# One weight load cut in two, and summing matmuls spread over four column tiles, in a fused adaLN + linear attention + GEGLU kernel

## The chip, the cores and the metric

The kernel runs on 1 core of one Trainium2 chip. The metric is device time in microseconds (us), median over runs. The profile of a kernel is one execution, and its span (first to last instruction) is usually 2.1 to 2.2 us shorter than the device time of the same run. PE is TensorE's matmuls, PEld its weight loads, DVE VectorE, ACT ScalarE, SP the engine whose queue issues the DMAs.

## The reference, cut to what matters

```python
mod = (silu(c) @ w_mod).reshape(1, 6, 1, -1)      # six rows of 1024
sa, ca, ga, sb, cb, gb = ...
h = layernorm(x) * (1 + ca) + sa                  # x: 2048 x 1024, bf16
x = x + ga * linear_attention(h, wqkv, wo)        # 32 heads, D = 1024
h = layernorm(x) * (1 + cb) + sb
x = x + gb * (gelu(h @ w_gate) * (h @ w_up) @ w_down)   # F = 3584
```

Two kinds of work come from `mod`. `sa` and `ca` are needed at once, before the first `k` matmul, as one value per partition. `ga`, `sb`, `cb` and `gb` are needed later, two of them (`ga`, `gb`) as rows copied to all partitions.

Of the kernel before, what the change touches and what calls it, by code (L numbers as in the profile page):

```python
# [7 lines left out]
ACTF = mybir.ActivationFunctionType  # L8
ALU = mybir.AluOpType

P = 128
# [203 lines left out]
def bass_adaLN_cond__linear_attn_block__geglu_ffn__prompt_kernel(  # L215
# [13 lines left out]
    scr_row = nc.dram_tensor("scr_row", [3, 4, 512], f32).ap()  # L229
    scr_rd = nc.dram_tensor("scr_rd", [NSG, 2, HPG, NG * (SGW // 2)], f32).ap()  # L230
    with ExitStack() as es:
# [3 lines left out]
        ps_all = es.enter_context(nc.psum_tensor("ps_all", [P, 8 * 512], f32))  # L235
# [75 lines left out]
        ONES, SILF, C8, CT, CHALF, THC, SILUT = (_small[k] for k in ("ones", "silf", "c8", "cT", "chalf", "thc", "siluT"))  # L311
# [5 lines left out]
        def r_sm(name):  # L317
            return [(SMO[name], SMO[name] + SMSZ[name], name)]
# [73 lines left out]
        def pr(b):  # L392
            return [(b * 2048, (b + 1) * 2048)]
# [7 lines left out]
        sch = Sched()  # L401
        T, A, V, G, Q = PE_, ACT_, DVE_, POOL_, SP_
# [11 lines left out]
        def pset_writer(b, o):  # L414
            for t_ in pr(b):
                sch.ps.set_writer(t_[0], t_[1], o)
# [30 lines left out]
        def w_dma(dst, off, name, kind, c0, c1, dc0=0, dc1=NDC):  # L447
            return sch.dma(Q, lambda e: e.dma_start(dst[:, dc0:dc1, c0:c1], wqkv_v[:, dc0:dc1, kind * D + c0:kind * D + c1]),  # L448
                           wr=[t_ for dc in range(dc0, dc1) for t_ in r_w(off, name, dc, c0, c1)], note=f"{name}.{dc0}.{c0}")

        def wmq_dma(q, ts=(0, 1)):
            for t in ts:
                sch.dma(Q, lambda e, t=t: e.dma_start(WMQ[q][:, :, t, :], wm_v[:, :, t * D + q * 256:t * D + (q + 1) * 256]),  # L453
                        wr=r_wmq(q, t), note=f"wmq{q}.{t}")
# [10 lines left out]
        x_dma(3, 4)  # L465
        for q in range(1, 4):
            wmq_dma(q)
            for d0, d1 in ((2, 4),) if q == 1 else ((2 * q, 2 * q + 1), (2 * q + 1, 2 * q + 2)):
                w_dma(WK, OFF_WK, "wk", 1, 0, D, d0, d1)
        w_dma(WV, OFF_WV, "wv", 2, 0, 512, 0, 4)  # L470
        w_dma(WV, OFF_WV, "wv", 2, 0, 512, 4, 8)
# [7 lines left out]
               rd=r_sm("c8") + r_sm("ident"), pwr=pr(4))  # L479
# [4 lines left out]
               rd=r_sm("thc") + r_sm("chalf"), wr=r_sm("siluT"))  # L484
# [152 lines left out]
        def mod_rows(parts):  # L637
            for k0, n, bank, src in parts:
                o = None
                for h in range(2):  # L640
                    for j in range(n):
                        ap, rng = src(k0 + j, h)
                        o = sch.op(T, lambda e, h=h, j=j, ap=ap, bank=bank: e.matmul(  # L643
                            ps_all[32 * j:32 * (j + 1), bank * 512:(bank + 1) * 512], ONES[:, :], ap, start=(h == 0), stop=(h == 1)),
                            rd=rng + r_sm("ones"), pwr=(pr(bank) if h == j == 0 else ()), note=f"modr{k0}.{h}.{j}")
                pset_writer(bank, o)

        def mod_store(n, bank, dst, rng, row):
            sch.op(A, lambda e: e.activation(dst[0:32 * n, :], ps_all[0:32 * n, bank * 512:(bank + 1) * 512], ACTF.Copy),
                   prd=pr(bank), wr=rng, note=f"mrow{row}")  # L650
            return sch.dma(Q, lambda e: e.dma_start(scr_row[row, 0:n, :], dst[0:32 * n:32, :]), rd=rng, note=f"mrow{row}.st")

        def hl_src(k, h):
            return HL[k // 4][:, k % 4, h, :], r_hl(k, h, h + 1)
# [57 lines left out]
        def nb():  # L712
            b = bank_i[0] % bank_i[1]
            bank_i[0] += 1
            return b
# [123 lines left out]
        for c_ in range(4):  # L839
            for vc, jg in (((0, 0), (1, 0)), ((0, 1), (1, 1)), ((2, 0), (2, 1)), ((3, 0), (3, 1)))[c_]:  # L840
                b = nb()
# [58 lines left out]
        for c_ in range(4, NCH):  # L900
# [23 lines left out]
            for jg in range(2):  # L924
                b = nb()
# [3 lines left out]
            for jg in range(2):  # L929
                b = nb()  # L930
# [3 lines left out]
            if c_ == 13:  # L934
                assert mdone[0] == 48 and not late
                b2_ = nb()
                mod_rows(((0, 2, 4, hl_src), (2, 4, b2_, hl_src)))
                o_r = mod_store(2, 4, MROW[0], r_2k(OFF_ROW, "mrow0"), 0)
                row_load(GAB, R_GAB, 0, 0, "gab", o_r)
                o_r = mod_store(4, b2_, MROW[1], r_2k(OFF_ROW + 2048, "mrow1"), 1)  # L940
                for dst, nt, a0 in ((SBT, "sbT", 0), (CBT, "cbT", 2)):
                    sch.dma(Q, lambda e, dst=dst, a0=a0: e.dma_start(dst[:, :], scr_row[1, a0:a0 + 2, :].rearrange("a (b p) -> p (a b)", p=P)),
                            wr=r_sm(nt), deps=[o_r], note=nt)
# [262 lines left out]
        def gb_rows():  # L1206
            mod_rows(((0, 2, 7, lambda j, h: (HLG[:, j, h, :], r_hlg(j, h))),))
            o_ = mod_store(2, 7, MRG, [(OFF_GAB, OFF_GAB + 2048, "mrg")], 2)
            row_load(GBB, R_GBB, 2, 0, "gbb", o_)
# [107 lines left out]
```

## The kernel before: what the change touches

At the start, one DMA queue (SP) brings in x, four "quarters" of the columns of `w_mod` for `sa` and `ca` (`wmq`), and the k weight (`wk`). A quarter holds two 128-row blocks `dc` of the contraction: TensorE can run the `k` matmuls of a `dc` only when the `wk` rows of that `dc` are there and the quarter's `wmq` have given `sa` and `ca` for it.

```python
x_dma(0, 1); x_dma(1, 2); wmq_dma(0, (1,)); x_dma(2, 3); wmq_dma(0, (0,))
w_dma(WK, OFF_WK, "wk", 1, 0, D, 0, 2)                       # wk, first quarter, one load
x_dma(3, 4)
for q in range(1, 4):
    wmq_dma(q)                                               # two loads of 512 KB
    for d0, d1 in ((2, 4),) if q == 1 else ((2 * q, 2 * q + 1), (2 * q + 1, 2 * q + 2)):
        w_dma(WK, OFF_WK, "wk", 1, 0, D, d0, d1)             # q == 1: one load of 512 KB
# ... (wv, x, wq)
# TensorE, in program order:
k_tiles([2, 3], [(0, 0), (0, 1), (1, 0), (1, 1)])            # first use of wk of the second quarter
# ...
mod_cols(2, 4)                                               # third quarter: waits for its wmq
# ...
mod_cols(3, 4)                                               # fourth quarter: waits for the last wmq
# ... the rest of the kernel
```

`mod_cols` is 32 matmuls of one column. The later rows of `mod` are summed on VectorE per partition, and TensorE adds over the partitions with a matmul by a 128 x 32 matrix of ones. I call the part of the array that such an output of 32 partitions uses (128*32 in the traces) a column tile; there are four, `j` picks one, and `h` adds the high and the low bf16 half of the sum.

```python
def mod_rows(parts):
    for k0, n, bank, src in parts:
        for h in range(2):
            for j in range(n):                 # n = 2: two column tiles; n = 4: all four
                ap, rng = src(k0 + j, h)
                o = sch.op(T, lambda e, ...: e.matmul(
                    ps_all[32 * j:32 * (j + 1), bank * 512:(bank + 1) * 512], ONES[:, :], ap,
                    start=(h == 0), stop=(h == 1)), ...)
        pset_writer(bank, o)

def mod_store(n, bank, dst, rng, row):
    sch.op(A, lambda e: e.activation(dst[0:32 * n, :], ps_all[0:32 * n, bank * 512:(bank + 1) * 512], ACTF.Copy), ...)
    return sch.dma(Q, lambda e: e.dma_start(scr_row[row, 0:n, :], dst[0:32 * n:32, :]), ...)
```

There are two sites: one in the k/v phase (a group of n = 2, then one of n = 4) and one at the end of the first feed-forward group (n = 2).

## Time and profile before

| | before |
|---|---|
| device time, median (3 runs) | 839.39 us (838.2 to 840.23) |
| profiled span | 835.7 us |
| TensorE busy | 829.8 us |

From the page of the kernel before: the span, the busy time of each engine, and the shares of the chain of work that ended last.

```profile
span 835.7 us, 11352 instructions
...
PE 829.8 (99%) x4189; PEld 384.2 (46%) x4189; DVE 512.3 (61%) x898; ACT 336.2 (40%) x555; POOL 36.7 (4%) x91
...
PE 97%; SPq 2%; DMA 1%; issue 0%; DVE 0%
```

The chain is TensorE (PE) nearly all the way. Here it is in order of time, kernel before; the columns are start, duration and what the chain went through.

```profile
17.27 1.51 SPq L453
18.83 5.91 DMA wmq<-in_w_mod_dram
24.78 0.95 PE ps_all L602 x32
...
151.80 0.97 PE ps_all L643 x12
...
348.98 0.54 PE ps_all L643 x4
```

Up to 24.78 us the chain is SP's issuing and then the last `wmq` load. From 24.78 us on, at the 32 matmuls of `mod_cols(3)` (L602), it is PE. I call this moment the *resume*. The ones matmuls (L643) are two pieces of that PE chain, 0.97 and 0.54 us.

All of PE's waits, kernel before (total us, times, longest):

```profile
PE ps_all L478 <- POOL bmask L429: 2.1, 1, 2.1
PE ps_all L602 <- DMA wmq<-in_w_mod_dram: 0.6, 2, 0.4
PE ps_all L680 <- DVE h1T L565: 0.5, 1, 0.5
```

The timeline of the kernel before around the second quarter's first `k` matmul, and the `mod_cols` of the third and fourth quarter; in brackets the idle time in front, with what seems to have ended it:

```profile
16.30 0.38 DVE L565 TENSOR_SCALAR h1T<-h1T,modt 128x384 bf16<-128x384 bf16 x1
...
17.02 2.53 PE L680 MATMUL ps_all<-wk,h1T 128*128 128x512 bf16 x11 [0.49 <-DVE h1T L565]
...
20.57 0.95 PE L602 MATMUL ps_all<-siluT,wmq 128*128 128x1 bf16 x32
...
24.78 0.95 PE L602 MATMUL ps_all<-siluT,wmq 128*128 128x1 bf16 x32 [0.21 <-DMA wmq<-in_w_mod_dram]
```

The list of DMA issues, limited to the window of the second quarter's `wk` load (issued at 8.62 us), kernel before; the last column is us from issue to landing:

```profile
wk<-in_A_wqkv_dram SPq DMA_DIRECT2D x1, 512.0 KB, 8.3
```

The load lands at 16.92 us. DVE's multiply for the first `dc` is done at 16.68, and PE starts at 17.02. So the profile's "DVE" as releaser is a near miss: the load came last.

The weight load of that first matmul, in the timeline of all engines, kernel before, and the last instruction of VectorE, whose end I call the *end* below:

```profile
16.99 2.07 PEld L680 LDWEIGHTS ps_all<-wk,h1T 128*128 128x128 bf16 x11 [0.64 <-DVE h1T L565]
...
833.54 0.22 DVE L1164 TENSOR_TENSOR xall<-ps_all,xall 128x64 bf16<-128x64 f32 x1
```

The ones matmuls of the kernel before, by form (minimum, median and maximum ns of one, then first and last start):

```profile
L643 PE MATMUL ps_all<-hl,ones x12: 379/379/391, 151.7 to 152.4; 128*32 128x512 bf16 x12
L643 PE MATMUL ps_all<-hlg,ones x4: 379/384/390, 348.9 to 349.1; 128*32 128x512 bf16 x4
```

### The profile page before, as it was taken

How to read it: one execution, taken by the hardware profiler on the slowest of the kernel's cores; microseconds unless marked ns; L12 is line 12 of the kernel's file. 1: busy time of each engine (PE TensorE's matmuls, PEld its weight loads, DVE VectorE, ACT ScalarE, POOL GpSimd, SP SyncE). 2: the span in 40 equal slices, each digit the busy share in tenths (PEclk: the TensorE clock that was granted, in tenths of full speed). 3: DMA queues.
4: the chain of work that ended last, by engine and by line, in shares of the span. 5: the costliest groups of instructions: out<-in, count | busy, mean ns of one | idle time of the engine just before them, and what ended most of it. 6: DMA issues, size and time to landing. Idle time of an engine off the chain costs nothing.

```text
span 835.7 us, 11352 instructions
## 1 busy us (share of the span) xinstructions
PE 829.8 (99%) x4189; PEld 384.2 (46%) x4189; DVE 512.3 (61%) x898; ACT 336.2 (40%) x555; POOL 36.7 (4%) x91
## 2 busy tenths in 40 slices
PE   8999999999999999999999999999999999999998
PEld 4544444444444444444444444444444444444445
DVE  6778877687785567753566665355556535555512
ACT  2357777446423354420444442045554104455300
POOL 2012111000200000000000000000000000000000
PEclk9999999999999999999999999999999999999999
DMA  9984323239796779180555533055553305555000
GB/s 284 332 240 120 83 76 84 70 88 227 151 234 194 227 210 275 26 188 26 158 151 151 152 101 75 20 158 152 151 151 102 76 20 161 153 154 143 7 19 26
DMA packets 184102, 113.22 MB, mean 135 GB/s; under 512 B 35560, under 2 KB 175080, under 8 KB 183024
## 3 DMA queue, kind: packets, MB, share of 16 engines
q1 hardware_dynamic: 184032, 112.50, 49.9%
q8 instruction: 33, 0.54, 0.3%
q14 instruction: 21, 0.17, 0.1%
q10 hardware_dynamic: 16, 0.00, 0.0%
HBM read 100.67 MB, written 4.47 MB: 126 GB/s over the span
## 4 chain that ended last, share of the span: by engine, by line
PE 97%; SPq 2%; DMA 1%; issue 0%; DVE 0%
PE ps_all L1157 23%; PE ps_all L1129 23%; PE ps_all L1132 23%; PE ps_all L680 12%; PE ps_all L1072 7%; PE ps_all L721 7%; SPq L448 1%; PE ps_all L702 1%; SPq L453 1%; DMA wmq<-in_w_mod_dram 1%; PE ps_all L974 0%; PE ps_all L986 0%; SPq L442 0%; PE ps_all L643 0%; PE ps_all L756 0%; PE ps_all L602 0%
## 5 line engine op out<-in xcount | busy, mean ns | idle before, releaser
L1129 PE MATMUL ps_all<-h2T,wg 128*128 128x512 bf16 x896 | 339.6, 379 | 0.0
L1132 PE MATMUL ps_all<-h2T,wu 128*128 128x512 bf16 x896 | 339.6, 379 | 0.0
L1157 PE MATMUL ps_all<-wd,yT 128*128 128x512 bf16 (+3 forms) x952 | 194.2, 366 | 0.0
L1140 ACT ACTIVATE q<-ps_all 128x512 f32<-128x512 f32 x112 | 66.9, 597 | 226.1 <-PE ps_all L1129 222.2
L1157 PEld LDWEIGHTS ps_all<-wd,yT 128*128 128x128 bf16 x952 | 90.1, 98 | 103.9 <-issue 0.4
L1129 PEld LDWEIGHTS ps_all<-h2T,wg 128*128 128x128 bf16 x896 | 87.7, 98 | 105.8 <-issue 0.2
L1132 PEld LDWEIGHTS ps_all<-h2T,wu 128*128 128x128 bf16 x896 | 87.7, 98 | 105.6
L1145 DVE SCALAR_TENSOR_TENSOR ww<-th,guh 128x512 f32<-128x512 f32 x112 | 77.5, 692 | 77.9 <-ACT th L1144 77.9
L1142 DVE SCALAR_TENSOR_TENSOR ww<-q,ps_all 128x512 f32<-128x512 f32 x112 | 76.9, 687 | 77.5 <-ACT guh L1141 77.5
L1144 ACT ACTIVATE th<-ww 128x512 f32<-128x512 f32 x112 | 70.5, 629 | 87.4 <-DVE ww L1142 87.4
L1162 DVE TENSOR_TENSOR ps_all<-ps_all,gbb 128x512 f32<-128x512 f32 (+3 forms) x34 | 22.7, 667 | 94.8 <-PE ps_all L1157 94.8
L1147 DVE TENSOR_TENSOR yT<-ww,ps_all 128x512 bf16<-128x512 f32 x112 | 76.9, 686 | 3.8
L1141 ACT ACTIVATE guh<-ps_all 128x512 f32<-128x512 f32 x112 | 66.2, 591 | 0.0
L721 PE MATMUL ps_all<-h1T,wq 128*128 128x512 bf16 x256 | 58.7, 379 | 0.0
L680 PE MATMUL ps_all<-wv,h1T 128*128 128x512 bf16 x256 | 57.7, 379 | 0.0
L669 ACT ACTIVATE eb<-ps_all 128x512 f32<-128x512 f32 x64 | 37.5, 599 | 49.7 <-PE ps_all L721 22.1
L680 PE MATMUL ps_all<-wk,h1T 128*128 128x512 bf16 x248 | 56.6, 379 | 0.5 <-DVE h1T L565 0.5
L1072 PE MATMUL ps_all<-w,pq 128*128 128x512 bf16 x256 | 56.2, 379 | 0.0
L670 DVE TENSOR_SCALAR eb<-eb 128x512 f32<-128x512 f32 x64 | 27.1, 424 | 26.4 <-ACT eb L669 26.0
L1072 PEld LDWEIGHTS ps_all<-w,pq 128*128 128x128 bf16 x256 | 25.0, 98 | 30.2 <-issue 0.2
L680 PEld LDWEIGHTS ps_all<-wv,h1T 128*128 128x128 bf16 x256 | 24.9, 98 | 29.5
L680 PEld LDWEIGHTS ps_all<-wk,h1T 128*128 128x128 bf16 x248 | 23.8, 98 | 28.8 <-DVE h1T L565 1.6
(96 smaller groups left out, 479.7 us busy)
## 6 DMA issues: line engine op xcount, KB each, us to landing
wg<-in_B_w_gate_dram SPq DMA_DIRECT2D x56, 512.0 KB, 4.1
wu<-in_B_w_up_dram SPq DMA_DIRECT2D x56, 512.0 KB, 5.3
rb<-scr_rd SPq DMA_DIRECT2D x32, 256.0 KB, 7.4
wd<-in_B_w_down_dram SPq DMA_DIRECT2D x7, 1024.0 KB, 8.7
wmst<-in_w_mod_dram SPq DMA_DIRECT2D x6, 1024.0 KB, 6.7
wmq<-in_w_mod_dram SPq DMA_DIRECT2D x8, 512.0 KB, 6.8
out_dram<-xall SPq DMA_DIRECT2D x31, 128.0 KB, 1.7
xall<-in_A_x_dram SPq DMA_DIRECT2D x3, 1024.0 KB, 11.9
```

Source lines behind the costliest of these rows:

```text
L680: o = sch.op(T, lambda e, dc=dc: e.matmul(PS(bank), H1[sg][:, dc, ci * P:(ci + 1) * P], W_[:, dc, jg * 512:(jg + 1) * 512], start=(dc == 0 ...
L721: o = sch.op(T, lambda e, dc=dc: e.matmul(PS(b), WQ[:, dc, qc * P:(qc + 1) * P], H1[sg][:, dc, :], start=(dc == 0), stop=(dc == NDC - 1)), ...
L1072: last[half] = sch.op(T, lambda e, g=g, half=half: e.matmul(PS(b0 + half), PQ[sg][:, g, ci * P:(ci + 1) * P], W2[:, g, half * 512:(half + ...
L1129: og = sch.op(T, lambda e, dc=dc: e.matmul(PS(bg), WG[slot][:, dc, e_ * P:(e_ + 1) * P], H2[sg][:, dc, :], start=(dc == 0), stop=(dc == ND ...
L1132: ou = sch.op(T, lambda e, dc=dc: e.matmul(PS(bu), WU[slot][:, dc, e_ * P:(e_ + 1) * P], H2[sg][:, dc, :], start=(dc == 0), stop=(dc == ND ...
L1140: sch.op(A, lambda e: e.activation(Q1[j][:, :], PS(bg), ACTF.Square, scale=math.sqrt(GELU_A)), prd=pr(bg), wr=rq, note=f"q1 {fc}")
L1141: ogh = sch.op(A, lambda e: e.activation(GUH[j][:, :], PS(bg), ACTF.Copy, scale=0.5), prd=pr(bg), wr=rg, note=f"gh {fc}")
L1142: sch.op(V, lambda e: e.scalar_tensor_tensor(WW[j][:, :], Q1[j][:, :], 1.0, PS(bg), op0=ALU.add, op1=ALU.mult), rd=rq, prd=pr(bg), wr=rw, ...
L1144: sch.op(A, lambda e: e.activation(TH[j][:, :], WW[j][:, :], ACTF.Tanh, scale=GELU_C), rd=rw, wr=rt, note=f"th {fc}")
L1145: sch.op(V, lambda e: e.scalar_tensor_tensor(WW[j][:, :], TH[j][:, :], 1.0, GUH[j][:, :], op0=ALU.add, op1=ALU.mult), rd=rt + rg, wr=rw, n ...
L1147: sch.op(V, lambda e: e.tensor_tensor(YT[:, fc, :], WW[j][:, :], PS(bu), ALU.mult), rd=rw, prd=pr(bu), wr=r_yt(fc), note=f"yT {fc}")
L1157: o = sch.op(T, lambda e, b=b, fc=fc, c0=c0, c1=c1, n=n: e.matmul(PS(b, 0, n), YT[:, fc, ci * P:(ci + 1) * P], WDT[fc // 4][:, fc % 4, c0:c1],
```

## The change

The intent: let TensorE start on the first `dc` of the second quarter while the second is still on its way; and let a group of two rows use all four column tiles, each with half the columns, so that the group takes half the array time. The copy out of PSUM gets half as wide too.

```diff
-            for d0, d1 in ((2, 4),) if q == 1 else ((2 * q, 2 * q + 1), (2 * q + 1, 2 * q + 2)):
+            for d0, d1 in ((2 * q, 2 * q + 1), (2 * q + 1, 2 * q + 2)):
                 w_dma(WK, OFF_WK, "wk", 1, 0, D, d0, d1)
...
         def mod_rows(parts):
             for k0, n, bank, src in parts:
                 o = None
+                w = n * P
                 for h in range(2):
-                    for j in range(n):
-                        ap, rng = src(k0 + j, h)
-                        o = sch.op(T, lambda e, h=h, j=j, ap=ap, bank=bank: e.matmul(
-                            ps_all[32 * j:32 * (j + 1), bank * 512:(bank + 1) * 512], ONES[:, :], ap, start=(h == 0), stop=(h == 1)),
+                    for j in range(4):
+                        ap, rng = src(k0 + j * n // 4, h)
+                        ap = ap[:, j * w % 512:j * w % 512 + w]
+                        o = sch.op(T, lambda e, h=h, j=j, ap=ap, bank=bank, w=w: e.matmul(
+                            ps_all[32 * j:32 * (j + 1), bank * 512:bank * 512 + w], ONES[:, :], ap, start=(h == 0), stop=(h == 1)),
...
         def mod_store(n, bank, dst, rng, row):
-            sch.op(A, lambda e: e.activation(dst[0:32 * n, :], ps_all[0:32 * n, bank * 512:(bank + 1) * 512], ACTF.Copy),
+            w = n * P
+            sch.op(A, lambda e: e.activation(dst[:, 0:w], ps_all[:, bank * 512:bank * 512 + w], ACTF.Copy),
...
-            return sch.dma(Q, lambda e: e.dma_start(scr_row[row, 0:n, :], dst[0:32 * n:32, :]), rd=rng, note=f"mrow{row}.st")
+            return sch.dma(Q, lambda e: e.dma_start(scr_row[row, 0:n, :].rearrange("a (h b) -> (a h) b", b=w), dst[0:128:32, 0:w]), rd=rng, note=f"mrow{row}.st")
```

For n = 4 the new code is the old one (w = 512); only the two groups with n = 2 change.

## The prediction

> **What bounds the kernel now.** Before: median 839.39 us (838.2 to 840.23). The page gives TensorE 829.8 of 835.7 us busy, clock 1.000; the chain that ended last is 97% PE. The list of PE waits holds about 3 us: 2.1 at the start, 0.6 for `wmq` loads, 0.5 for `h1T`. So only removed PE time, or an earlier landing of the load PE waits for last, shortens the run. That load is the last `wmq` quarter: the chain follows SP's issues to 18.83 us, then 5.91 us of this load; PE goes on at 24.78 and waits for no load again.
>
> **Part 1: wk of the second quarter in two loads.** The 512 KB load is issued at 8.62 us (3.43 us in SP) and lands 8.3 us later, at 16.92; PE's first matmul with it starts at 17.02 after 0.49 us idle. The list names DVE (`h1T`), but the first DVE multiply ended by about 16.65, so I read the load as the releaser. Split, its first half should land 0.5 to 0.8 us earlier (256 KB at the 310 to 330 GB/s of these stretches, an estimate), and PE start at about 16.7, 0.3 us earlier. But PE then waits for `wmq` of the third quarter (resumes at 20.57) and the fourth (24.78). DMA engines are at full share from about 5 us on, and the bytes ahead of these loads are the same; one more issue costs about 0.45 us of SP (short ones take 0.43 to 0.47), which SP should have, as its long issues (2.4 to 3.4 us) look like waits for room. The 0.3 us turns into a longer wait for `wmq`. Worth: 0 us, between -0.2 and +0.3.
>
> **Part 2: half-width ones matmuls.** A two-tile group has 4 matmuls of 512 columns on two column tiles; after, 8 of 256 on four. The Trainium skill ("TensorE: Matmul & The Clock Gate", Part 3) says that matmuls on different column tiles run concurrently, and the trace agrees: 32 of 256 columns on four tiles (the `den` group) take 0.99 us of the chain, 31 ns each, though one lasts 273 ns. The group at 348.98 takes 0.54 us of the chain: two waves of 512 columns (0.215 us each, the spacing of the large matmuls) and about 0.11 us of switching. After: two waves of 0.107, so 0.33. The site at 151.80 (12 matmuls, 0.97 us) keeps its four-tile group and should take 0.76. Both lie on PE's chain: together -0.42 us.
>
> The ACT copy goes from 64x512 (0.59 and 0.57 us) to 128x256, about 0.38 (an estimate); the store writes four rows of 1 KB instead of two of 2 KB. They feed `gab` and `gbb`, read by DVE; PE waits for neither. Worth 0.
>
> **Prediction.** 839.39 - 0.4, about 838.9 us; 8 in 10 between 837.8 and 840.1, a width that is run-to-run spread. Faster by over 2%: 0.003; within 2%: 0.994; slower by over 2%: 0.003.
>
> **What would show it.** Right: ones matmuls are 16 of 256 columns and 8 of 512; their chain pieces are 0.7 to 0.8 and 0.3 to 0.37 us; the wait before the first second-quarter `wk` matmul shrinks by about 0.3 us, and PE still resumes after the last `wmq` within 0.3 us of 24.78. Wrong: pieces still 0.97 and 0.54 (weight loads or issue bound small matmuls), or the last `wmq` landing moved by over 0.3 us.
>
> **What would make it wrong.** The extra load pushing the `wmq` landings back by up to its issue time, 0.5 us; or the shifted order of queue slots giving PE a new wait later.

## The result, and the profile after

| | before | after |
|---|---|---|
| device time, median (6 runs each) | 838.81 us (837.82 to 840.23) | 838.31 us (837.44 to 840.14) |
| ratio after to before | | 0.9994, 95% interval 0.9979 to 1.0009 |
| profiled span | 835.7 us | 835.8 us |

Ratios here are the mean time of one kernel's fast runs over that of the other's of the same rounds, so they are not quite the ratio of the medians quoted. The two kernels are the same within 2%, and the interval holds 1. The times alone don't tell whether 0.4 us was gained. The traces tell what each part is worth.

From the page of the kernel after:

```profile
span 835.8 us, 11370 instructions
...
PE 829.0 (99%) x4197; PEld 384.0 (46%) x4197; DVE 512.2 (61%) x898; ACT 335.9 (40%) x555; POOL 36.9 (4%) x91
...
PE 97%; SPq 2%; DMA 1%; issue 0%; DVE 0%
```

There are eight more matmuls (4197 against 4189): the two groups of four became two of eight. The chain in order of time, kernel after (L645 is the old L643):

```profile
16.93 8.25 DMA wmq<-in_w_mod_dram
25.23 0.95 PE ps_all L602 x32
...
152.25 0.76 PE ps_all L645 x16
...
349.23 0.33 PE ps_all L645 x8
```

The pieces of the ones matmuls shrank from 0.97 to 0.76 us and from 0.54 to 0.33 us. But the resume moved from 24.78 to 25.23 us, which cancels the 0.42 us. All of PE's waits, kernel after:

```profile
PE ps_all L478 <- POOL bmask L429: 2.1, 1, 2.1
PE ps_all L602 <- DMA wmq<-in_w_mod_dram: 1.6, 2, 1.5
PE ps_all L683 <- DVE h1T L565: 0.2, 1, 0.2
```

The same places of the timeline, kernel after:

```profile
15.58 0.38 DVE L565 TENSOR_SCALAR h1T<-h1T,modt 128x384 bf16<-128x384 bf16 x1
...
16.02 2.55 PE L683 MATMUL ps_all<-wk,h1T 128*128 128x512 bf16 x11 [0.20 <-DVE h1T L565]
...
21.08 0.95 PE L602 MATMUL ps_all<-siluT,wmq 128*128 128x1 bf16 x32 [1.46 <-DMA wmq<-in_w_mod_dram]
...
25.23 0.95 PE L602 MATMUL ps_all<-siluT,wmq 128*128 128x1 bf16 x32 [0.16 <-DMA wmq<-in_w_mod_dram]
```

Now DVE really is the releaser: its multiply ends at 15.96 and PE starts at 16.02. The wait there fell by 0.29 us, and the next one, for the third quarter's `wmq`, grew to 1.46 us. The same weight load and the last instruction of VectorE, kernel after:

```profile
16.02 2.06 PEld L683 LDWEIGHTS ps_all<-wk,h1T 128*128 128x128 bf16 x11 [0.37 <-DVE h1T L565]
...
833.58 0.22 DVE L1167 TENSOR_TENSOR xall<-ps_all,xall 128x64 bf16<-128x64 f32 x1
```

The ones matmuls of the site at 152 us, by form:

```profile
L645 PE MATMUL ps_all<-hl,ones x16: 272/331/379, 152.2 to 152.6; 128*32 128x256 bf16 x8, 128*32 128x512 bf16 x8
```

Two readings of the later resume are open: it is caused by the extra load, or it is scatter between two single traces. The experiments begin there.

### The profile page after: what moved, and what is told of

The parts are those of the page before. It is cut to its first block, busy times and chain, and to the rows that moved or that the text cites. A ratio compares the mean times of both kernels' runs of the same rounds, so it can differ in the third digit from the quotient of the medians.

```text
span 835.8 us, 11370 instructions
## 1 busy us (share of the span) xinstructions
PE 829.0 (99%) x4197; PEld 384.0 (46%) x4197; DVE 512.2 (61%) x898; ACT 335.9 (40%) x555; POOL 36.9 (4%) x91
## 4 chain that ended last, share of the span: by engine, by line
PE 97%; SPq 2%; DMA 1%; issue 0%; DVE 0%
PE ps_all L1160 23%; PE ps_all L1132 23%; PE ps_all L1135 23%; PE ps_all L683 12%; PE ps_all L1075 7%; PE ps_all L724 7%; SPq L448 1%; DMA wmq<-in_w_mod_dram 1%; PE ps_all L705 1%; SPq L453 1%; PE ps_all L977 0%; PE ps_all L989 0%; SPq L442 0%; PE ps_all L645 0%; PE ps_all L759 0%; PE ps_all L602 0%
```

## The experiments

All kernels gave correct results.

### One part at a time, and each kernel a second time

**e1_wk_only**: the kernel before with the first line of the diff only.

> The kernel before with the wk split alone. My theory (the split is worth nothing, because TensorE next waits for a modulation load whose bytes ahead are unchanged, and the start scatters by some tenths of a us from run to run): ratio to before 1.000 within 0.15%; the resume after the last wmq wait lies within the scatter of the unsplit kernels of this set. Rival (the extra load pushes the wmq landings back by its issue time, about 0.45 us, as the one trace after suggests: 25.23 against 24.78 us): resume at 25.1 to 25.3 us, later than every unsplit kernel, time +0.4 us.

**e2_ones_only**: the kernel after with that line put back.

```diff
-            for d0, d1 in ((2 * q, 2 * q + 1), (2 * q + 1, 2 * q + 2)):
+            for d0, d1 in ((2, 4),) if q == 1 else ((2 * q, 2 * q + 1), (2 * q + 1, 2 * q + 2)):
```

> The kernel before with the half-width ones matmuls alone. My theory: chain pieces of the ones matmuls 0.76 and 0.33 us, as in the trace after (before: 0.97 and 0.54), the start as before, time -0.4 us (ratio 0.9995, which the interval can't tell from 1). If the wk split was the loss, this kernel is faster than both.

**e3_before_again**: no edit.

> The kernel before, unchanged, as a second look: measures the scatter. Ratio 1.000 within 0.15%. My theory: the resume after the last wmq wait differs from 24.78 us by some tenths with no change to the kernel. Rival: it stays within 0.1 us of 24.78.

**e4_after_again**: no edit.

> The kernel after, unchanged, as a second look. My theory: ratio about 0.9995; the resume after the last wmq wait anywhere from 24.5 to 25.3 us. Rival: again about 25.2 us, as it comes from the extra load.

Measured, five runs each against nine of the kernel before (837.88 us):

| | median us | ratio to before (95%) |
|---|---|---|
| e1_wk_only | 838.34 | 1.0006 (0.9992 to 1.0020) |
| e2_ones_only | 838.07 | 1.0002 (0.9989 to 1.0014) |
| e3_before_again | 838.44 | 1.0007 (0.9994 to 1.0020) |
| e4_after_again | 837.64 | 0.9998 (0.9985 to 1.0010) |

No time differs from 1. The unchanged kernel (e3) is off by 0.07%, more than the effect sought. The traces, though, can be cut at the resume. In this table "end" is the end of the last VectorE add (its start plus its duration); the last column is the difference of the two columns before it. The later experiments are included. The wait is that of the weight load (PEld): the traces of e1 to e4 lack 80 matmul records each (4109 or 4117 where the kernels have 4189 or 4197), the first matmul of this place among them, so PE's own waits there (0.43, 0.68, 0.64 and 0.43 us) are about 0.22 us too long. The weight loads are complete.

| trace | wk loads | ones groups of two | weight load's wait before the second quarter's first wk matmul | third-quarter wmq | resume | end | end - resume |
|---|---|---|---|---|---|---|---|
| before | 6 | wide | 0.64 | 20.57 | 24.78 | 833.76 | 808.98 |
| e3_before_again | 6 | wide | 0.57 | 21.12 | 25.31 | 834.30 | 808.99 |
| e5_rep_wide | 6 | (repeated) | 0.60 | 20.75 | 24.94 | | |
| e7_rep_cut | 6 | (repeated) | 0.63 | 20.49 | 24.63 | | |
| e2_ones_only | 6 | half | 0.61 | 20.92 | 25.10 | 833.67 | 808.57 |
| e1_wk_only | 7 | wide | 0.37 | 20.76 | 25.14 | 834.13 | 808.99 |
| after | 7 | half | 0.37 | 21.08 | 25.23 | 833.80 | 808.57 |
| e4_after_again | 7 | half | 0.38 | 20.80 | 24.93 | 833.51 | 808.58 |
| e6_rep_half | 7 | (repeated) | 0.38 | 20.50 | 24.67 | | |

Three things follow.

1. From the resume to the end these traces hardly scatter: 808.98 or 808.99 us with the wide ones matmuls, 808.57 or 808.58 with the half-width ones, whichever way the wk load is cut. Part 2 is worth 0.41 us, to a hundredth.
2. The resume scatters by 0.68 us over five traces with the wk load whole (24.63 to 25.31, mean 24.95) and by 0.56 us over four with it cut (24.67 to 25.23, mean 24.99). The third-quarter `wmq` comes at a mean of 20.77 and 20.79 us. So no shift by the split is seen. These few traces can't exclude a small one: with a standard deviation of about 0.26 us in each group, the means (0.04 us apart) are known to about 0.4 us either way. But 0.45 us between two traces needs no cause in the change: unchanged, the kernel before resumed at 24.78 once and at 25.31 the other time. The rival of e1 said that a kernel with seven loads resumes later than every unsplit one; e4 (24.93) and e6 (24.67) don't, so it falls in that form, and so does its claim in e3 that an unchanged kernel stays within 0.1 us. What makes the resume scatter is open.
3. The split does what it was meant to do where it acts: the weight load's wait before the second quarter's first wk matmul is 0.57 to 0.64 us in the five traces whole and 0.37 or 0.38 in the four cut, 0.24 us less on average; e8 to e11, also cut, show 0.37 or 0.38 too. That gain ends at the next wait. (When the first half landed the profile doesn't say, so the forecast 0.5 to 0.8 us for it is not checked.)

The chain pieces of e2_ones_only show part 2 alone:

```profile
152.12 0.76 PE ps_all L645 x16
...
349.10 0.33 PE ps_all L645 x8
```

### Is it the four tiles, or the shorter matmuls?

To see 0.2 us in the time, the group at 349 us was issued 51 times instead of once. The repeats write the same sums, so results stay right.

**e5_rep_wide**, on the kernel before:

```diff
-                for h in range(2):
+                for h in list(range(2)) * (51 if bank == 7 else 1):
```

> The kernel before with its second ones group (two column tiles, 4 matmuls of 512 columns) issued 51 times in place of once; the repeats write the same sums again. Theory: each repeat costs two waves of 512 columns, 0.43 us, so +21.5 us (+2.6%), and the group's piece of the chain is about 22 us.

**e6_rep_half**, the same edit on the kernel after.

> The kernel after with its second ones group (four column tiles, 8 matmuls of 256 columns) issued 51 times. My theory: each repeat costs two waves of 256 columns, 0.215 us, so about +10.7 us against the kernel after (+1.3%). Rival (weight loads or issue bound such short matmuls): more than 31 ns for each, 0.25 us or more for a repeat, +12.5 us or more.

**e7_rep_cut**: on the kernel before, matmuls cut to 256 columns, but still on two tiles; each half finishes its sum before the next half starts in that bank.

```diff
-                for h in range(2):
-                    for j in range(n):
-                        ap, rng = src(k0 + j, h)
+                for s, h in [(s, h) for s in range(2 if n == 2 else 1) for h in range(2)] * (51 if bank == 7 else 1):
+                    for j in range(n):
+                        ap, rng = src(k0 + j, h)
+                        w = 256 if n == 2 else 512
+                        ap = ap[:, s * w:(s + 1) * w]    # output columns s * w to (s + 1) * w of the bank
```

> The kernel before with its two-tile ones groups cut in halves of 256 columns but left on two column tiles, the second group issued 51 times. Tells whether the width or the four tiles bring the gain. My theory (only matmuls on different column tiles overlap): each repeat is four waves of 256 columns, 0.43 us, +21.5 us like the wide one. Rival (shorter matmuls alone are the gain): +10.7 us like the four-tile one.

The piece of the chain in order of time that holds the repeated group, in e5_rep_wide:

```profile
349.14 22.12 PE ps_all L643 x204
```

The same piece in e6_rep_half:

```profile
348.67 11.25 PE ps_all L645 x408
```

And in e7_rep_cut:

```profile
348.84 22.38 PE ps_all L645 x408
```

| | tiles | columns of one | us for one repeat, from the chain | median us (before 838.45) | ratio to before |
|---|---|---|---|---|---|
| e5_rep_wide | 2 | 512 | (22.12 - 0.54) / 50 = 0.432 | 859.91 | 1.0256 |
| e6_rep_half | 4 | 256 | (11.25 - 0.33) / 50 = 0.218 | 850.14 | 1.0137 |
| e7_rep_cut | 2 | 256 | (22.38 - 0.54) / 50 = 0.437 | 860.19 | 1.0259 |

The four tiles bring the whole gain. Cutting the matmuls without using more tiles brings none (0.437 against 0.432 us). The same 408 matmuls take 54.6 ns each on two tiles and 27.3 ns each on four (22.38 and 11.25 us less the first group, over 400), which also answers the rival of e6: 27 ns, not 31. A wave of 512 columns takes 0.215 us, so four matmuls of 256 columns at once make 27 ns each (an estimate): neither the weight loads nor the issue of 408 pairs held them up beyond that.

One miss: I expected e6 at about 10.7 us above the kernel after, and its median lies 11.7 above the kernel before of the same rounds, where with its gain of 0.4 us (the other site) it should be near 10.5. Its four runs are not alike. The one at clock 1.000 took 849.01 us, 10.6 above, as expected. Two (850.73 and 850.38) show a mean clock of 0.998, of which more below, and the first of them spent 2.8 us outside its span. The profiled one (849.91) has the TensorE piece as expected (11.25 us), but its last store took 3.0 us to land where the kernel before needed 1.4. Why that store was late is open.

### More loads still

**e8_wk_eight**: the kernel before, with the second and the first quarter of wk in two loads each.

```diff
-        w_dma(WK, OFF_WK, "wk", 1, 0, D, 0, 2)
+        w_dma(WK, OFF_WK, "wk", 1, 0, D, 0, 1)
+        w_dma(WK, OFF_WK, "wk", 1, 0, D, 1, 2)
... (and the line of the second quarter as in the diff of the change)
```

> The kernel before with wk in eight loads of 256 KB (first and second quarter split): two issues more than before, one more than after, same bytes and same rows. My theory: resume after the last wmq wait in the scatter of the others (24.5 to 25.3 us). Rival (each extra issue costs 0.45 us): about 25.7 us.

Measured: 839.25 us, ratio 1.0005 (0.9988 to 1.0022). Its profiled run resumed at 26.91 us, later than both theories allow. From its timeline of PE:

```profile
21.40 0.95 PE L603 MATMUL ps_all<-siluT,wmq 128*128 128x1 bf16 x32 [1.38 <-DMA wmq<-in_w_mod_dram]
22.21 4.87 PE L681 MATMUL ps_all<-wk,h1T 128*128 128x512 bf16 x14
26.91 0.95 PE L603 MATMUL ps_all<-siluT,wmq 128*128 128x1 bf16 x32
```

No load released that resume: the last `wmq`, issued at 17.31 us, had landed 8.2 us later, at 25.51. The third quarter's `wmq` came at 21.40 us after a wait of 1.38 us, and then the granted TensorE clock was at half for 3.41 us, in which PE was busy without a gap. From the resume to the end this trace took 808.98 us, like every trace with wide ones matmuls. Two of its four runs show a mean clock of 0.998 and took 840.04 and 840.20 us; the other two, at 1.000, took 838.19 and 838.47. A half-clock stretch of 3.41 us loses 1.7 us, and that is the size of this difference. Without the stretch the profiled run would have resumed soon after 25.51, near the rival's 25.7, so this trace alone doesn't decide between the theories. The two runs at 1.000 speak for mine: their spans, 836.0 and 836.3 us, lie among those of the kernel before in the same rounds (835.6 to 836.5 at 1.000), where the rival's two more issues would add 0.9 us. Not every run at 0.998 is slow: one of e3 took 838.81 us where its others took 838.06 to 838.93. Single runs of the kernels before and after also have clock 0.998 at times (1 of 6 of after, 840.14 us). (The mean alone doesn't tell where the clock fell: the trace of e6 shows 0.999, from a stretch after its last matmul, which costs nothing.) This deserved its own test, because a split that gathers PE's waiting in one place might bring it on.

### The half-clock stretch

**e9_long_wait**: the kernel after with one wv load moved ahead of the third quarter's `wmq`.

```diff
         for q in range(1, 4):
+            if q == 2:
+                w_dma(WV, OFF_WV, "wv", 2, 0, 512, 0, 4)
             wmq_dma(q)
...
-        w_dma(WV, OFF_WV, "wv", 2, 0, 512, 0, 4)
```

> The kernel after with the first wv load (512 KB) moved ahead of the third quarter's wmq loads, so that TensorE's wait for them grows from about 1.4 to about 3 us. Every later modulation load is 1.6 us later, so the resume moves by +1.6 us by the load alone. My theory for the runs of clock 0.998 (such as the wk_eight trace, 23.2 to 26.9 us): a wait at this place, with the 32 one-column matmuls after it, can drop the granted clock to half for 3.4 us. Then most runs here show clock 0.998 and the time is +3 us or more. Rival (the half-clock stretches are unrelated to the wait): +1.6 us, clock 1.000 in most runs.

**e10_long_wait_fill**: the same, with dummies.

```diff
         k31([2, 3])
+        warm(11)            # 11 matmuls of zeros into an open sum (comment mine)
         mod_cols(2, 4)
```

> The same as the long wait, with 11 dummy matmuls of 512 columns (zeros added into an open sum) ahead of the third quarter's modulation matmuls: 2.4 us of TensorE work inside the wait. My theory: clock 1.000 in all runs, time +1.6 us against the kernel after, so 1.5 us or more less than with the empty wait. Rival: same as the empty wait or slower by the dummies.

**e11_after_fill**: the kernel after with `warm(4)` in that place.

> The kernel after with 4 dummy matmuls (0.86 us) in the same place, inside the wait of 1.0 to 1.5 us. My theory: the resume after the last wmq stays in 24.6 to 25.3 us and no run shows clock 0.998, so the median is that of the kernel after within 0.1% and the slow single runs near 840 us are gone. This is the candidate to beat both kernels, by less than the interval shows. Rival (dummies only delay the chain): +0.5 us or more.

The timeline of PE in e9_long_wait (where the added line moves L602 to L603):

```profile
22.40 0.95 PE L603 MATMUL ps_all<-siluT,wmq 128*128 128x1 bf16 x32 [2.09 <-DMA wmq<-in_w_mod_dram]
23.21 4.87 PE L684 MATMUL ps_all<-wk,h1T 128*128 128x512 bf16 x14
27.92 0.94 PE L603 MATMUL ps_all<-siluT,wmq 128*128 128x1 bf16 x32
```

One line of the view by stretches of e9_long_wait: start and end, length, then busy us and count of PE, PEld, DVE, ACT and POOL; the last three numbers are the granted clock, the DMA share and GB/s.

```profile
24.00:26.00 2.00, 2.00 (x7) 0.81 (x6) 0.51 (x2) 0.00 (x0) 0.00 (x0) 0.50 1.03 299
```

The timeline of PE in e10_long_wait_fill:

```profile
20.09 2.54 PE L740 MATMUL ps_all<-warm 128*128 128x512 bf16 x11
22.46 0.94 PE L603 MATMUL ps_all<-siluT,wmq 128*128 128x1 bf16 x32
23.26 3.18 PE L684 MATMUL ps_all<-wk,h1T 128*128 128x512 bf16 x14
26.28 0.94 PE L603 MATMUL ps_all<-siluT,wmq 128*128 128x1 bf16 x32
```

And the same stretch of e10_long_wait_fill:

```profile
24.00:26.00 2.00, 2.00 (x11) 0.97 (x10) 0.56 (x2) 0.00 (x0) 0.00 (x0) 1.00 1.05 357
```

The `wmq` matmuls start at the same time (22.40 and 22.46 us). After the empty wait the next 14 matmuls take 4.87 us at half clock for most of it; with dummies in the wait, 3.18 us at full clock. The resume differs by 1.64 us. (With dummies it is 26.28 us, 1.3 us after the mean of the kernels with seven loads, for the load moved ahead.)

| | runs at clock 0.998 | median us | spans of the runs, us | ratio to before (95%) |
|---|---|---|---|---|
| e9_long_wait | 3 of 5 | 840.16 | 838.4, 838.6, 838.0 at 0.998; 837.1, 836.8 at 1.000 | 1.0017 (1.0003 to 1.0030) |
| e10_long_wait_fill | 0 of 5 | 839.96 | 836.8, 837.9, 837.0, 837.2, 836.8 | 1.0017 (1.0005 to 1.0030) |
| e11_after_fill | 0 of 5 | 837.89 | 836.1 at most, 835.3 at least | 0.9994 (0.9981 to 1.0006) |

Empty waits were followed by the half-clock stretch in the traces of e8 and e9, and with dummies in the wait no run showed it. Five runs each are few: 3 of 5 against 0 of 5 points to the wait as the cause and doesn't settle it. Nor does the length of the wait decide: in the kernel after, PE waited 1.46 us at the same place, longer than in e8, and in e1 1.68 us before the `wmq` matmuls at 10.62 us, and the clock stayed at 1.000 in both traces. In the spans the dummies gain 1.0 us by the medians (838.0 to 837.0); in the device times they don't, since three runs of e10 spent 0.7 to 1.1 us more than the usual 2.1 us outside the span. Why is open, and my forecast of 1.5 us or more less than e9 was missed. The wait grew by less than I had expected (2.09 us, not 3), and the stretch came in 3 of 5 runs.

This agrees with the Trainium skill, "TensorE: Matmul & The Clock Gate", Part 1, which gives a free-running window of 3413 ns for the clock gate: the clock records of e8 and e9 both show half clock for 3.413 us, and a window that isn't tied to the kernel's start would explain why only some runs are hit. The clock records kept in the traces fit such a grid: full clock lasts 829.439 us in the kernel before, 243.00 times 3.4133 us, and a whole number of such windows (243 to 250) in every trace without a stretch at the start; in e8 and e9 the stretch begins 17.067 us, five windows, after full clock was first granted. That first moment lies between 5.62 us (e7) and 7.88 us (e4) of the span. In the window that ended as the stretch began, PE was busy 2.11 of 3.41 us (e8) and 1.62 (e9); in the kernel after, whose wait lies across a border of the grid, 2.53. That how busy PE is within one window decides is argued, not shown: a window of e1 (9.07 to 12.48 us) has 1.81 us busy, two matmul records short, and no drop follows.

e11 resumes at 25.18 us and ends 808.57 us later, like the other kernels with half-width ones matmuls. It beats neither kernel beyond the interval. With a stretch in about one run of six or fewer, five runs can't show that it is gone.

## Why the prediction was right

The time lay in the range (838.31 us against 837.8 to 840.1), and "the same within 2%" held. Neither tests the mechanism: the kernel before, unchanged, lies in that range too (838.81 us). The stated 838.9 was 0.6 us high, more than the effect, because its base of 839.39 us was the median of three runs; from 838.81, the median of six, the forecast gain of 0.42 gives 838.39. What tests the mechanism is the traces. Point by point:

- **TensorE's chain bounds the kernel.** Shown: the end follows the resume by the same 808.57 or 808.98 us in ten traces of kernels without repeated groups (all those in the table above, and e8 to e11).
- **Part 2, -0.21 us at each site, -0.42 together.** Shown: pieces 0.76 and 0.33 us as forecast, -0.41 us from resume to end. The `den` group that the estimate was checked on has the same shape, 256 columns on four tiles. The copy out of PSUM went from 0.59 and 0.57 us to 0.38 and 0.37 us at the two sites (ScalarE), as estimated, and PE's list of waits has no new entry.
- **Part 1, 0.3 us less wait that turns into a longer wait for `wmq`.** The first half is shown (PE's wait 0.49 to 0.20 us in the first two traces; the weight load's 0.61 to 0.37 on average), and it is 0.24 to 0.29 us. The second half is supported in sum, as the resume doesn't move on average (24.95 and 24.99 us, known to about 0.4 us); in a single trace the `wmq` wait depends on when the loads come.
- **The extra issue costs nothing.** No cost is seen, with seven loads or, in the two runs at full clock, with eight; a cost of a few tenths of a us isn't excluded.
- **A criterion that failed.** I had written that a `wmq` landing moved by over 0.3 us would show me wrong. It moved by 0.45 us in the trace after, and I wasn't. The criterion took one trace for the kernel's own time: the unchanged kernel moves by 0.53 us between two traces.
- **The width of the range.** It was put down to run-to-run spread. The runs show two parts of that spread: the resume, and the half-clock stretch, 1.7 us in the trace of e8, which I had not seen coming.

## What to carry to other kernels

When one engine is the chain from some moment to the end, measure from that moment: two traces cut there showed 0.41 us to a hundredth, where some ten timed runs of each kernel could not. Splitting a load is of use when the wait it shortens is the last one for data; here the next load swallowed it. Check that a trace has all its records before you compare waits: here 80 missing ones made a steady gain of 0.24 us look like scatter. Matmuls with outputs of 32 partitions were worth spreading over all four column tiles (0.432 to 0.218 us); shortening them on the same tiles gained nothing (0.437).

## What the Trainium skill lacked or had wrong

- "TensorE: Matmul & The Clock Gate", Back-to-back issue gap: it gives about 131 ns for each matmul of 512 columns in a stream of weight loads and matmuls. Here such streams run at 216 ns (16 matmuls in 3.45 us of the chain), the figure that this section keeps for the isolated case (Part 1 of the page has it as measured back to back, so the page disagrees with itself).
- The same page, Part 1 and the table of goals: it asks for idle gaps over about 3 us before the clock falls. Here waits of 1.38 us (e8) and 2.09 us (e9), and the 32 one-column matmuls after them, were followed by 3.413 us at half clock in the profiled runs; with the wait filled none of 5 runs showed it. In e6 the clock fell 2.0 us after the last matmul. (The page also tells of an oscillation through frequent short idles, its second failure mode, without a length.)
- The same page, Part 3: it has single packs only (2.38 times for three column tiles). In a steady stream, going from two tiles to four halves the time per matmul of 256 columns, 54.6 to 27.3 ns. And no page has a time for entering and leaving this mode: a group here takes 0.11 us more than one of its repeats does (0.54 against 0.43 us, and 0.33 against 0.22).
- The same page, LDWEIGHTS: its rule, columns over 1.2, would give 27 ns for 32 columns (an estimate). The trace records 93 to 97 ns for the 32-column loads, and about as much for 128 columns (98 ns). That doesn't refute the rule as a pace, because recorded durations can overlap: in e6 pairs of a load and a matmul follow each other every 27.3 ns.
